# One small transfer from GpSimd's queue ahead of the setup of a fused attention and gated-MLP kernel

## The chip, the cores and the metric

The kernel runs on one core of a Trainium2 chip. The core has a matrix engine (TensorE, PE in the profile, with its weight loads as PEld), a vector engine (VectorE, DVE), an activation engine (ScalarE, ACT), a general engine (GpSimd, POOL) and a queue engine (SyncE, SP) that here only issues transfers. Each engine works through its own instructions in order and waits on semaphores for the others. Transfers run on 16 DMA engines; SP and ACT issue them on hardware queues, GpSimd on a software queue. The metric is the device time of one execution in microseconds, as the median of several runs; less is better.

## The reference

Layer norm, a sliding-window attention with dilation, a residual; layer norm, a ReLU-gated MLP, a residual. S = 2048 rows, D = 512, 32 heads of 16, window 8 with step 2, F = 1376, all in bfloat16:

```python
def _A_ref(x, wqkv, wo):
    qkv = (x @ wqkv).reshape(B, S, 3, H, Dh).transpose(2, 0, 3, 1, 4)
    q, k, v = qkv[0], qkv[1], qkv[2]
    idx = pos[:, None] - (jnp.arange(8) * 2)[None, :]
    ...
    logits = jnp.where(mask, jnp.einsum("bhsd,bhswd->bhsw", q, kg) * Dh ** -0.5, -1e9)
    o = jnp.einsum("bhsw,bhswd->bhsd", _softmax(logits), vg)
    return o.transpose(0, 2, 1, 3).reshape(B, S, D) @ wo

def _B_ref(x, W_gate, W_up, W_down):
    gate, up = x @ W_gate, x @ W_up
    return (gate * (gate > 0) * up) @ W_down

h = x + _A_ref(_layernorm(x), A_wqkv, A_wo)
out = h + _B_ref(_layernorm(h), B_W_gate, B_W_up, B_W_down)
```

## The kernel before

The 2048 rows are worked in four chunks of 512 (`tk`), each of four blocks of 128 rows (`j`). For each chunk: layer norm of x with rows on the partitions, transposes on PE (L518), projections to q, k, v with features on the partitions (L559, copied out by ACT at L567), products of q with the shifted k on DVE (L608, or L623 for the first chunk), their sums per head on PE (L614), exponentials on ACT, the weights spread to all partitions (over PE and ACT for the first chunk at L743 and L749, by SP's transfers at L732 for the others), products with the shifted v on DVE (L764, L779), a tree of sums of which the first level is an accumulating transfer of GpSimd's queue (L807, for chunks 0 to 2) and the rest is on DVE (L767, L771, L801), the output projection (L833), the second layer norm, gate and up (L906, L910, L913, L934) and down (L952, L963), and the store (L969).

The order of the work is fixed before the program is built. A planner class takes about 740 steps with an engine, an estimated duration and a rank from a table (`RANK`), lays them out and emits the instructions in that order, so that steps of several chunks interleave on each engine. No scheduler moves them afterwards; semaphore waits are placed between them by the framework.

Ahead of the planned steps stands `setup()`, in the order of its lines, and this is where the change lies:

- x of the first chunk is loaded in four transfers of 128 KB, by SP and ACT in turn (L309), then the q and k columns of the weights, `wqk_sb`, in four transfers of 256 KB (L311), one for each 128 of the 512 rows of `A_wqkv`; a row of that tensor has 3 x 512 elements, 3072 bytes. Then SP loads x of the second chunk (L312).
- DVE zeroes `warm` (L314). PE multiplies it 44 times into a bank that nobody reads (L408), and 8 times more after each of the first two transposed blocks (L416).
- GpSimd makes `identity` (two instructions of a helper), `eps_t` (L316), `ci`, the number of each partition (L317), four more index tables (L318 to L321) and the zero pads of `kT` and `vT` (L322, L323).
- GpSimd copies one element of x into `wv_sb` (L326) once the first x block has landed, which holds back SP's load of the v columns, `wv_sb` (L327), until then; a second copy of this kind (L328) holds back SP's loads of the other two x chunks (L330) and all weights behind them (L332 to L338) until x of the second chunk is there.
- DVE makes the constants `sel`, `spread`, `same` and `mask` from `ci` and the tables (L343 to L351).

After that come the planned steps, on DVE first those of the first layer norm: statistics of each x block (L454), their aggregate (L457), a logarithm and an exponential on ACT (L467, L471), the normalised rows (L489), a transpose on PE (L518), and a copy out of the bank by ACT (L534) or, for every second block, by DVE (L532). The first two projections to q and two to k run in halves: rows 0 to 255 of the weights against the first 256 x rows as soon as two blocks are copied out, and so on.

A transfer from GpSimd's queue is one instruction in GpSimd's order. Its landing is signalled on one of eight semaphores that these transfers use in turn.

Of the kernel before, what the change touches and what calls it, by code (L numbers as in the profile page):

```python
# [8 lines left out]
P = 128  # L9
BF16 = mybir.dt.bfloat16  # L10
# [81 lines left out]
class Plan:  # L92
# [9 lines left out]
    def add(self, key, *a, **k):  # L102
        op = Op(*a, **k)
        op.key = key
        op.seq = len(self.ops)
        if RANK:
            op.prio = RANK[op.seq]
        self.ops.append(op)
        for b in set(op.take) | set(op.use):
            b.left += 1  # L110
        return op
# [97 lines left out]
def kernel(  # L209
# [11 lines left out]
    nc = tc.nc  # L221
# [4 lines left out]
    NT = D // P  # L226
# [24 lines left out]
    sb = ctx.enter_context(tc.tile_pool(name="sb", bufs=1))  # L251
# [10 lines left out]
    mask = sb.tile([P, 2, PADL], BF16, name="mask")  # L262
    eps_t = sb.tile([P, 1], F32, name="eps_t")
    warm = sb.tile([P, P], BF16, name="warm")
    ci = sb.tile([P, 1], I32, name="ci")
    tmp = sb.tile([P, 3], I32, name="tmp")
    cf = sb.tile([P, 4], F32, name="cf")
# [37 lines left out]
    def setup():  # L305

        w3_r = A_wqkv.rearrange("(dt p) f -> p dt f", p=P)
        for j in range(BPC):
            (nc.scalar if j % 2 else nc.sync).dma_start(x_sm[:, j:j + 1, :], x_rows[:, j:j + 1, :])  # L309
        for dt in range(NT):  # L310
            (nc.scalar if dt % 2 else nc.sync).dma_start(wqk_sb[:, dt:dt + 1, :], w3_r[:, dt:dt + 1, 0:2 * D])  # L311
        nc.sync.dma_start(x_sm[:, BPC:2 * BPC, :], x_rows[:, BPC:2 * BPC, :])  # L312
        nc.scalar.preload_act_table_set("natural_log_exp_and_others")
        V.memset(warm[:], 0.0)  # L314
        make_identity(nc, identity[:])
        nc.gpsimd.memset(eps_t[:], EPS)  # L316
        nc.gpsimd.iota(ci[:], pattern=[[0, 1]], base=0, channel_multiplier=1)  # L317
        nc.gpsimd.iota(sel_i[:], pattern=[[1, H]], base=0, channel_multiplier=0)  # L318
        nc.gpsimd.iota(sp_i[:], pattern=[[1, H], [0, DQ]], base=0, channel_multiplier=0)
        nc.gpsimd.iota(sm_i, pattern=[[0, 4], [1, H]], base=0, channel_multiplier=0)  # L320
        nc.gpsimd.iota(mk_i[:], pattern=[[1, PADL]], base=0, channel_multiplier=0)  # L321
        nc.gpsimd.memset(kT[:, :, 0:PADL], 0.0)  # L322
        nc.gpsimd.memset(vT[:, :, 0:PADL], 0.0)  # L323


        nc.gpsimd.tensor_copy(out=wv_sb[0:1, 0, 0:1], in_=x_sm[0:1, 0, 0:1])  # L326
        nc.sync.dma_start(wv_sb[:], w3_r[:, :, 2 * D:3 * D])  # L327
        nc.gpsimd.tensor_copy(out=x_sm[0:1, 2 * BPC, 0:1], in_=x_sm[0:1, BPC, 0:1])  # L328
        for tk in range(2, NCK):
            nc.sync.dma_start(x_sm[:, tk * BPC:(tk + 1) * BPC, :], x_rows[:, tk * BPC:(tk + 1) * BPC, :])  # L330

        nc.sync.dma_start(wo_sb[:], A_wo.rearrange("(p t) f -> p t f", t=NT))  # L332
        nc.sync.dma_start(wgu_sb[:, :, 1, :], B_W_up.rearrange("(dt p) f -> p dt f", p=P))
        nc.sync.dma_start(wgu_sb[:, :, 0, :], B_W_gate.rearrange("(dt p) f -> p dt f", p=P))
        nc.sync.dma_start(
            wd_sb[:, 0:NFF, :], B_W_down[0:NFF * P, :].rearrange("(ft p) n -> p ft n", p=P))
        if FTAIL:
            nc.sync.dma_start(wd_sb[:FTAIL, NFF, :], B_W_down[NFF * P:F, :])  # L338


        for n, (op, by) in enumerate(((ALU.arith_shift_right, 2), (ALU.bitwise_and, H - 1),
                                      (ALU.arith_shift_right, 5))):
            V.tensor_scalar(out=tmp[:, n:n + 1], in0=ci[:], scalar1=by, scalar2=None, op0=op)  # L343
        V.tensor_copy(out=cf[:, 0:3], in_=tmp[:])
        V.tensor_scalar(out=cf[:, 2:3], in0=cf[:, 2:3], scalar1=1.0 * DIL, scalar2=None, op0=ALU.mult)
        V.tensor_scalar(out=cf[:, 3:4], in0=cf[:, 2:3], scalar1=4.0 * DIL, scalar2=None, op0=ALU.add)
        V.tensor_scalar(out=sel[:], in0=sel_i[:], scalar1=cf[:, 0:1], scalar2=None, op0=ALU.is_equal)
        V.tensor_scalar(out=spread[:], in0=sp_i[:], scalar1=cf[:, 1:2], scalar2=None, op0=ALU.is_equal)
        V.tensor_scalar(out=same[:], in0=sm_i, scalar1=cf[:, 1:2], scalar2=None, op0=ALU.is_equal)
        for hf in range(2):  # L350
            V.tensor_scalar(out=mask[:, hf, :], in0=mk_i[:], scalar1=cf[:, 2 + hf:3 + hf],  # L351
                            scalar2=None, op0=ALU.is_ge)
# [189 lines left out]
    for tk in range(NCK):  # L542
# [10 lines left out]
        for n, (c, t) in enumerate(seq):  # L553
# [16 lines left out]
            if tk == 0 and n < 4:  # L570

                ab, done = [wload["ab"]], []
                for i, (lo, hi, evs) in enumerate(((0, 2 * P, xev[0:2]), (2 * P, CS, xev[2:]))):
# [3 lines left out]
                a = add(("qkd%d" % n, tk), "PE", 2 * MM, lambda f=f_mm: f(0, CS, 2, NT), done + [wl], pr - 4.9, take=[mm],  # L577
                        use=[xnT], lat=PEL)
            else:
                a = add(("qkv%d" % n, tk), "PE", 4 * MM, f_mm, xev + [wl], pr, take=[mm], use=[xnT], lat=PEL)  # L580
# [13 lines left out]
        for hf in range(2):  # L594
            sc, ex = Buf(at_s), Buf(ex_s)
            scd, prd = [], []
            for t in range(0, NT, 2):
# [20 lines left out]
                if tk in PRS:  # L618
# [7 lines left out]
                    for u in range(2):  # L626
                        a = add(("pr%d%s" % (hf, "ac"[u]), tk), "DVE", D20, lambda u=u, f=f_p1: f(u),
                                [d[t + u] for d in (qd, kd, kp)], apr, take=[pb], use=[qT], lat=DL)
                        prd.append((a, pb, f_sc if u else lambda: None))
                else:  # L630
                    a = add(("pr%d" % hf, tk), "DVE", D40, f_pr, [d[k] for k in (t, t + 1) for d in (qd, kd, kp)],
                            apr, take=[pb], use=[qT], lat=DL)
                    prd.append((a, pb, f_sc))
            if (tk, hf) in PRD:
                def f_pd(p0=prd[0][1], p1=prd[1][1]):
                    nc.gpsimd.dma_start(p0.t[:], p1.t[:], accum_op=ALU.add, max_dma_last_dim=4096)

                a = add(("pd%d" % hf, tk), "POOL", 1.3, f_pd, [a for a, _, _ in prd], apr, use=[b for _, b, _ in prd],
                        lat=1.1, dq=(0.75, 5.48))
# [9 lines left out]
            elif (tk, hf) in PRE:  # L649
# [3 lines left out]
                a = add(("pa%d" % hf, tk), "DVE", D40, f_pa, [a for a, _, _ in prd], apr, use=[b for _, b, _ in prd], lat=DL)  # L653
# [24 lines left out]
            a = add(("ex%d" % hf, tk), "ACT", A5, f_ex, scd, apr, take=[ex], use=[sc], lat=AL)  # L678
            if tk == 0:
                a = add(("mk%d" % hf, tk), "DVE", DSM, f_mk, [a], apr, use=[ex], lat=DL)  # L680
# [41 lines left out]
        for w0 in range(0, W, BCN):  # L722
# [23 lines left out]
            a = add(("bc%d" % hf, tk), "PE", MM + SW, f_bc, [exd[hf]], apr + 1, take=bcs, use=[exs[hf]], lat=PEL)  # L746
# [9 lines left out]
        for t in range(NT):  # L756
# [46 lines left out]
            for n, du in ((4, D20), (2, D10), (1, D2)):  # L803
                f = lambda n=n, mt=mt, f=f_a: f(n, mt)
# [23 lines left out]
        for j in range(BPC):  # L828
# [10 lines left out]
            def f_rs(j=j, od=od, sm=sm, tk=tk):  # L839
# [3 lines left out]
                else:  # L843
# [3 lines left out]
            a = add(("wo%d" % j, tk), "PE", (5 if tk in RPE else 4) * MM, f_wo, list(oev.values()) + [wload["o"]],  # L847
                    base + 50, take=[od], use=[OT], lat=PEL)
            if tk in RPE:
                a = add(("rs%d" % j, tk), "ACT", 0.57, f_rs, [a], base + 50, take=[sm], use=[od], lat=AL)  # L850
            else:
                a = add(("rs%d" % j, tk), "DVE", 0.63, f_rs, [a], base + 50, take=[sm], use=[od], lat=DL)
# [7 lines left out]
        for f0 in range(0, NFT, 2):  # L860
            fts = range(f0, min(f0 + 2, NFT))
            if tk in TMT and fts[-1] == NFF:
# [4 lines left out]
                for b in range(2):  # L867
# [13 lines left out]
                    def f_tg(b=b, bk=bk, ht=ht, gr=gr):  # L881
# [4 lines left out]
                    a = add(("mm%d" % (f0 // 2), tk), "PE", 8 * TTM, f_tt, hev + [wload["u"], wload["g"]], mb + f0 * 0.1,  # L886
                            take=[bk], use=[hnT], lat=PEL)
                    a = add(("ge%d" % (f0 // 2), tk), "ACT", ATE, f_te, [a], mb + f0 * 0.1 - 200, take=[gr], use=[bk], lat=AL)
# [10 lines left out]
            for ft in fts:  # L899
# [15 lines left out]
                def mm(g, b, wl, pr=pr, f0=f0, ft=ft, f=f_mm, hnT=hnT):  # L915
                    if (tk, ft) not in HSP:
                        return add(("mm%d" % (f0 // 2), tk), "PE", 4 * MM, lambda: f(g, b), hev + [wload[wl]], pr,
                                   take=[b], use=[hnT], lat=PEL)
                    a = None
                    for i, (lo, hi, evs) in enumerate(((0, 2 * P, hev[0:1]), (2 * P, CS, hev[1:]))):  # L920
                        a = add(("mm%d%s" % (f0 // 2, "ac"[i]), tk), "PE", 2 * MM + 0.005, lambda lo=lo, hi=hi: f(g, b, lo, hi),
                                evs + [wload[wl], a], pr, take=[b], use=[hnT], lat=PEL if i else 0.0)
                    return a

                a = mm(1, um, "u")
# [11 lines left out]
            a = add(("gu%d" % (f0 // 2), tk), "DVE", D10 if n == 2 else D2, f_gu, eds, pr - 200, take=[gt], use=[ub, gr], lat=DL)  # L937
# [7 lines left out]
        for n, (j, c0, c1) in enumerate(parts):  # L945
# [25 lines left out]
            a = None  # L971
            for lo, hi in ((0, 8), (8, NFT)):
                a = add(("dn%d" % n, tk), "PE", (hi - lo + (hi == NFT and tk in OPE)) * MM * share,
                        lambda lo=lo, hi=hi, f=f_dn: f(range(lo, hi)),
                        [gds[ft] for ft in range(lo, hi)] + [wload["d"], a], mb + 5, take=[od],
                        use=[gts[ft] for ft in range(lo, hi)], lat=PEL if hi == NFT else 0.0)
# [5 lines left out]
    with tc.manual_schedule():  # L982
        setup()
        for op in todo:
            if op.fn is not None:
                op.fn()
# [35 lines left out]
```

## Time and profile before

| | |
|---|---|
| median of 3 runs | 198.1 us (198.0 to 198.31) |
| span of the profiled execution, first to last instruction | 196.6 us |
| PE busy | 190.5 us, 97% of the span |
| DVE busy | 154.0 us, 78% |
| ACT busy | 111.7 us, 57% |
| POOL busy | 12.7 us, 6% |
| DMA moved | 21.99 MB in 21134 packets, 112 GB/s on average |
| granted TensorE clock | 1.00 |

The profile is one execution; its span leaves out some 1.5 us that the timed runs have around it. An engine's busy time counts what it computes; POOL's also counts its issuing of transfers, which it does in software. A row of a time line has the start from the span's beginning, the duration, the engine, the line and what is written from what; the brackets tell how long the engine stood idle before and what ended that. A matmul is listed with its whole passage through the array, so rows overlap, and the pitch from one to the next is what it costs. Some matmul records, here 20 of 1131, are missing.

### The profile page before, as it was taken

The numbers are of one execution on the slowest core, as the hardware profiler recorded it, in microseconds if no ns is written. First come the engines' busy times: TensorE is split into PE (matmuls) and PEld (weight loads), VectorE is DVE, ScalarE is ACT, GpSimd is POOL, SyncE is SP. The second block draws the span as 40 slices with busy tenths as digits, with TensorE's granted clock in tenths as the row PEclk, the third lists the DMA queues.
The fourth block names the chain that finished last, engine by engine and source line by source line (L and its number), as shares of the span: only waits on it lengthen the run. The fifth ranks groups of instructions, "written<-read, shape, count | busy, mean of one in ns | idle before, by whom it ended". The sixth has DMA issues, their size and how long they took to land.

```text
span 196.6 us, 3034 instructions
## 1 busy us (share of the span) xinstructions
PE 190.5 (97%) x1111; PEld 97.1 (49%) x1131; DVE 154.0 (78%) x251; ACT 111.7 (57%) x234; POOL 12.7 (6%) x28
## 2 busy tenths in 40 slices
PE   7899999999999999999999999999999999999994
PEld 7756445654445434464444435444444655444542
DVE  6779999999999999999999779999686331223233
ACT  3548699984598947694334658505674615235400
POOL 4000000330000013100033000000000000000000
PEclk9999999999999999999999999999999999999999
DMA  6969980695000809947369971411002220030114
GB/s 154 310 202 389 405 262 2 122 198 108 3 0 6 196 15 173 188 89 169 81 130 198 181 204 64 82 29 24 3 0 53 53 57 0 0 107 0 27 57 133
DMA packets 21134, 21.99 MB, mean 112 GB/s; under 512 B 8736, under 2 KB 17920, under 8 KB 21120
## 3 DMA queue, kind: packets, MB, share of 16 engines
q1 hardware_dynamic: 18672, 14.65, 25.9%
q0 software_dynamic: 1728, 6.29, 17.2%
q10 hardware_dynamic: 720, 0.85, 1.4%
q8 instruction: 9, 0.15, 0.3%
q14 instruction: 5, 0.04, 0.1%
HBM read 8.42 MB, written 2.10 MB: 53 GB/s over the span
## 4 chain that ended last, share of the span: by engine, by line
PE 66%; DMA 14%; issue 13%; DVE 4%; POOL 1%; SPq 1%; POOLq 0%; DVEq 0%
PE bank L906 20%; PE bank L559 19%; PE bank L952 14%; DMA big<-big 7%; PE bank L833 5%; DMA wv_sb<-in_A_wqkv_dram 4%; PE bank L614 2%; DVE big L764 2%; PE bank L873 2%; PE bank L518 2%; DMA x_sm<-in_A_x_dram 1%; POOL big L807 1%; DMA big<-ex 1%; DVE big L608 1%; PE bank L836 1%
## 5 line engine op out<-in xcount | busy, mean ns | idle before, releaser
L906 PE MATMUL bank<-quad,wgu_sb 128*128 128x512 bf16 x313 | 72.0, 379 | 0.4
L906 PEld LDWEIGHTS <-wgu_sb 128*128 128x128 bf16 x320 | 31.0, 98 | 37.3 <-issue 0.8
L952 PE MATMUL bank<-wd_sb,gT 128*128 128x512 bf16 (+2 forms) x182 | 40.1, 366 | 0.3
L913 ACT ACTIVATE gr<-bank 128x512 bf16<-128x512 f32 x40 | 23.2, 603 | 26.0 <-PE bank L906 24.5
L910 ACT CAST up_sb<-bank 128x512 bf16<-128x512 f32 x40 | 23.2, 594 | 16.5 <-PE bank L906 14.0
L934 DVE TENSOR_TENSOR gT<-gr,up_sb 128x1024 bf16<-128x1024 bf16 x20 | 13.7, 689 | 22.7 <-ACT up_sb L910 16.8
L559 PE MATMUL bank<-quad,wqk_sb 128*128 128x512 bf16 (+1 forms) x132 | 30.2, 367 | 0.2
L952 PEld LDWEIGHTS <-gT 128*128 128x128 bf16 (+1 forms) x187 | 18.1, 98 | 19.5 <-issue 0.4
L764 DVE TENSOR_TENSOR big<-big,vT 128x4096 bf16<-128x4096 bf16 x12 | 27.0, 2283 | 0.1
L608 DVE TENSOR_TENSOR big<-quad,kT 128x4096 bf16<-128x4096 bf16 x12 | 27.0, 2284 | 0.0
L559 PEld LDWEIGHTS <-wqk_sb 128*128 128x128 bf16 x136 | 14.7, 114 | 13.0 <-issue 2.1
L963 DVE TENSOR_TENSOR row<-x_sm,bank 128x512 bf16<-128x512 bf16 (+1 forms) x17 | 10.8, 651 | 9.2 <-PE bank L952 9.2
L767 DVE TENSOR_TENSOR big<-big 128x1024 bf16<-128x1024 bf16 (+2 forms) x24 | 16.8, 729 | 1.2 <-DMA big<-big 1.2
L559 PE MATMUL bank<-quad,wv_sb 128*128 128x512 bf16 x62 | 15.7, 380 | 0.4 <-DMA wv_sb<-in_A_wqkv_dram 0.3
L807 POOL DMA_DIRECT2D big<-big x12 | 10.5, 874 | 85.0 <-DVE big L764 55.0
L833 PE MATMUL bank<-wo_sb,quad 128*128 128x512 bf16 x62 | 14.7, 379 | 0.4 <-DVE quad L801 0.3
L489 DVE TENSOR_SCALAR row<-x_sm,mv,rs 128x512 bf16<-128x512 bf16 x32 | 11.4, 407 | 1.8 <-ACT rs L471 1.8
L534 ACT COPY quad<-bank 128x1024 bf16<-128x1024 bf16 (+1 forms) x11 | 10.0, 944 | 4.5 <-PE bank L518 4.4
L567 ACT CAST kT<-bank 128x512 bf16<-128x512 f32 x16 | 8.9, 598 | 5.7 <-PE bank L559 5.5
L454 DVE BATCH_NORM_STATS2 st<-x_sm 128x6 f32<-128x512 bf16 x16 | 10.3, 675 | 2.1 <-DMA x_sm<-in_A_x_dram 2.1
L567 ACT CAST quad<-bank 128x512 bf16<-128x512 f32 x16 | 9.5, 607 | 3.6 <-PE bank L559 3.6
L443 ACT ACTIVATE row<-x_sm,mv 128x512 bf16<-128x512 bf16 x12 | 8.6, 714 | 4.2 <-DVE mv L435 4.0
(72 smaller groups left out, 157.5 us busy)
## 6 DMA issues: line engine op xcount, KB each, us to landing
big<-big POOLq DMA_DIRECT2D x12, 512.0 KB, 5.4
big<-ex SPq DMA_DIRECT2D x24, 128.0 KB, 2.7
out_dram<-row SPq DMA_DIRECT2D x15, 128.0 KB, 1.8
x_sm<-in_A_x_dram SPq DMA_DIRECT2D x3, 512.0 KB, 4.9
wgu_sb<-in_B_W_up_dram SPq DMA_DIRECT2D x1, 1376.0 KB, 8.8
wgu_sb<-in_B_W_gate_dram SPq DMA_DIRECT2D x1, 1376.0 KB, 11.8
wd_sb<-in_B_W_down_dram SPq DMA_DIRECT2D x1, 1280.0 KB, 15.2
wqk_sb<-in_A_wqkv_dram SPq DMA_DIRECT2D x2, 256.0 KB, 6.9
```

The lines of the kernel that those rows point to most:

```text
L559: nc.tensor.matmul(mm.t[:, lo:hi], lhsT=wv_sb[:, dt, t:D:NT] if c == 2 else wqk_sb[:, dt, c * D + t:(c + 1) * D:NT], rhs=xnT.t[:, dt, lo:h ...
L567: nc.scalar.copy(out=o, in_=mm.t[:])
L608: V.tensor_tensor(out=pb.t[:].rearrange("p (t w) s -> p t w s", t=2), in0=q4, in1=k4, op=ALU.mult)
L764: V.tensor_tensor(out=mt.t[:], in0=ab.t[:], in1=v8, op=ALU.mult)
L767: V.tensor_tensor(out=mt.t[:, 0:n, :], in0=mt.t[:, 0:n, :], in1=mt.t[:, n:2 * n, :], op=ALU.add)
L807: nc.gpsimd.dma_start(mt.t[:, 0:4, :], mt.t[:, 4:8, :], accum_op=ALU.add)
L833: nc.tensor.matmul(od.t[:], lhsT=OT.t[:, t, j * P:(j + 1) * P], rhs=wo_sb[:, t, :], start=(t == 0), stop=(t == NT - 1 and tk not in RPE))
L906: nc.tensor.matmul(mm.t[:fs, lo:hi], lhsT=wgu_sb[:, dt, g, ft * P: ft * P + fs], rhs=hnT.t[:, dt, lo:hi], start=(dt == 0), stop=(dt == NT ...
L910: nc.scalar.copy(out=ub.t[:fs, i, :], in_=um.t[:fs, :])
L913: nc.scalar.activation(out=gr.t[:fs, i, :], in_=gm.t[:fs, :], func=ACT.Relu)
L934: V.tensor_tensor(out=gt.t[:fs, 0:n, :], in0=gr.t[:fs, 0:n, :], in1=ub.t[:fs, 0:n, :], op=ALU.mult)
L952: nc.tensor.matmul(od.t[:, c0:c1], lhsT=gts[ft].t[:fs, ft % 2, j * P:(j + 1) * P], rhs=wd_sb[:fs, ft, c0:c1], start=(ft == 0), stop=(ft == ...
```

## The change

A tile `touch` of 128 partitions by 2 elements is added, and as the first instruction of `setup()` GpSimd issues a transfer into it: from each of the 128 groups of four rows of `A_wqkv` the first two elements of the first row, 4 bytes. The source rows are 12288 bytes apart and run over the whole tensor. Nothing reads `touch`. On GpSimd's queue the transfer stands ahead of `identity`; on the other engines the instructions and their order are the same. The new tile takes 32 bytes of each partition, so the tiles allocated after it lie 32 bytes higher. The later transfers of GpSimd's queue take the next of the eight semaphores each.

```diff
@@ -262,6 +262,7 @@
     mask = sb.tile([P, 2, PADL], BF16, name="mask")
     eps_t = sb.tile([P, 1], F32, name="eps_t")
     warm = sb.tile([P, P], BF16, name="warm")
+    touch = sb.tile([P, 2], BF16, name="touch")
     ci = sb.tile([P, 1], I32, name="ci")
@@ -305,6 +306,7 @@
     def setup():
 
         w3_r = A_wqkv.rearrange("(dt p) f -> p dt f", p=P)
+        nc.gpsimd.dma_start(touch[:], A_wqkv.rearrange("(p a) f -> p a f", a=NT)[:, 0, 0:2])
         for j in range(BPC):
             (nc.scalar if j % 2 else nc.sync).dma_start(x_sm[:, j:j + 1, :], x_rows[:, j:j + 1, :])
```

## The prediction

> **What bounds the kernel now.** I read the page first, for which engine is full; then the waits, for whether the full engine ever stands still; then the time lines of the first 14 us, engine by engine, because the only edit is the first instruction of GpSimd's queue.
>
> ```profile
> PE 190.5 (97%) x1111; PEld 97.1 (49%) x1131; DVE 154.0 (78%) x251; ACT 111.7 (57%) x234; POOL 12.7 (6%) x28
> PE   7899999999999999999999999999999999999994
> DVE  6779999999999999999999779999686331223233
> ```
>
> PE is full from the second slice (4.9 us each) to the end, DVE from the fourth to past 100 us. The first slices are the ramp: until the first projections PE runs matmuls on zeros (L408, L416) and a few transposes. From the waits, all that PE itself waits for in the run:
>
> ```profile
> PE bank L408 <- DVE warm L314: 1.0, 1, 1.0
> PE bank L518 <- DVE row L489: 0.6, 2, 0.3
> PE bank L833 <- DVE quad L801: 0.3, 1, 0.3
> PE bank L559 <- DMA wv_sb<-in_A_wqkv_dram: 0.3, 1, 0.3
> ```
>
> Columns: microseconds in total, times, longest. The first two are in the ramp. The last, before 12.22 us, is no wait: the block that begins at 8.76 us is 16 matmuls of 256 columns (0.109 apart) and 8 of 512 (0.216 apart), 3.47 us, so it ends at 12.23; the row below has 21 of the 24, the rest are missing records. So after 8.76 us PE never stands still but 0.33 us at 115.25. What sets the time is when the first projection starts, plus a block of PE work that has no holes. What sets that start is read on POOL, then DVE, then PE:
>
> ```profile
> 0.74 0.21 POOL masks.py:197 MEMSET identity<- 128x128 bf16 x1 [0.29 <-POOLq L1006]
> 1.30 0.14 POOL L317 IOTA ci<- 128x1 int32 x1
> 2.30 0.15 POOL L323 MEMSET vT<- 128x64 bf16 x1
> ...
> 34.72 1.01 POOL L807 DMA_DIRECT2D big<-big  x1 [23.65 <-DVE row L489]
> 37.11 0.86 POOL L807 DMA_DIRECT2D big<-big  x1 [1.38 <-PE bank L518]
> ```
> ```profile
> 1.47 0.27 DVE L343 TENSOR_SCALAR tmp<-ci 128x1 int32<-128x1 int32 x3 [0.54 <-POOL ci L317]
> ...
> 2.83 0.36 DVE L351 TENSOR_SCALAR mask<-big,cf 128x16 bf16<-128x16 int32 x2
> 3.37 0.69 DVE L454 BATCH_NORM_STATS2 st<-x_sm 128x6 f32<-128x512 bf16 x1 [0.17 <-DMA x_sm<-in_A_x_dram]
> ...
> 8.20 0.75 DVE L532 COPY quad<-bank 128x512 bf16<-128x512 bf16 x2
> 10.87 1.88 DVE L454 BATCH_NORM_STATS2 st<-x_sm 128x6 f32<-128x512 bf16 x3 [1.92 <-DMA x_sm<-in_A_x_dram]
> ```
> ```profile
> 8.33 0.40 PE L518 MATMUL bank<-identity,row 128*128 128x128 bf16 x4
> 8.76 3.21 PE L559 MATMUL bank<-quad,wqk_sb 128*128 128x256 bf16 x21
> ```
>
> (Columns: start, duration, engine, line, what; in brackets the idle time before it and what ended it.) POOL's constants run without a hole from 0.74 to 2.45. DVE stands until ci comes (1.44), makes the constants until 3.19, waits 0.17 for the first x rows, and is then full but for 0.30 us until the copy of the second transposed row block ends at 8.58, and that releases the first projection at 8.76. The weights for it (rows 0 to 255 of the q and k part) have landed at 8.31 in the semaphores of their two transfers, 0.27 earlier: close, but not last.
>
> **The change part by part.** *The transfer's hold on POOL.* It stands before the identity, so every POOL instruction of the setup moves behind it: identity, eps_t, ci, the four iotas, the two pads of kT and vT, and the copies L326 and L328. The trace has no small transfer on this queue; the nearest rows are the twelve L807 ones, also 128 rows each. From release to start each takes about half a microsecond, then 0.86 (first one 1.01) on POOL:
>
> ```profile
> 74.94 0.02 POOLq L807
> 74.96 0.47 issue
> 75.43 0.02 POOLq L807
> 75.45 0.86 POOL big L807
> ```
>
> So 0.51 + 1.01 (it will be the first of its queue) = 1.52 us. Bounds: below, nothing, if POOL hands the work on and goes to the memset at once (never seen: each L807 is followed by a wait of over 1 us); next, 0.86 if the half microsecond overlaps the start of the program; above, 0.57 + 1.01 = 1.58, the time from the wait's end (34.15) to the first L807's end. I take 1.52: same engine, same row count, first use.
>
> The Trainium skill bears on this: "DMA: Bandwidth & Descriptors", section "Anatomy of one DMA — SWDGE (gpsimd) path", puts most of the fixed 2 us into the receipt of the write at the end, and little into dispatch and descriptor generation; by it the estimated hold is about 0.1 us and the sum is nought. The rows above, with 0.86 us booked on POOL itself, speak against it, and I go by the rows.
>
> *What waits.* DVE's L343 is blocked on ci, and DVE takes its work in order, so behind it stand all constants, the statistics of the first four x blocks, their normalisation and both L532 copies. ci comes at 1.44 + 1.52 = 2.96, the constants end at 4.71, and the first statistics start there instead of at 3.37 (the 0.17 wait is used up): 1.52 - 0.17 = 1.35 us late. The rest of the stretch to 8.58 is DVE's own chain with ACT's logarithm and exponential inside it, all of which moves; the first projection starts at 8.76 + 1.35 = 10.11. The other POOL results have room: identity at 2.8 for a transpose at 6.1, eps_t at 2.8 for ACT at 4.4. L326 goes from 3.40 to about 3.97, so SP's wv load (L327) is issued some 0.15 later than 4.05; SP's older x load is still landing until 10.84 ahead of it, and wv is now wanted at 13.6, not 12.2. L328 waits for x at 10.89 as before.
>
> *The transfer itself.* 128 packets of 4 bytes beside 21134. They come after about 0.7 + 1.5 + 0.6 = 2.8 us (the first L807 ends at 35.73, its first packet is at 36.29), among the first x blocks, which land between 3.3 and 5.0. If they hold x up by less than 1.35 us the later DVE start covers it.
>
> *What it may give.* The load rate shows a stretch where the weights' first packets crawl:
>
> ```profile
> 3.00:3.50 0.50, 0.50 (x7) 0.50 (x6) 0.33 (x3) 0.50 (x1) 0.10 (x1) 1.00 1.04 363
> 4.50:5.00 0.50, 0.50 (x7) 0.50 (x6) 0.47 (x2) 0.38 (x2) 0.00 (x0) 1.00 1.18 166
> 5.00:5.50 0.50, 0.50 (x8) 0.50 (x6) 0.50 (x2) 0.36 (x2) 0.00 (x0) 1.00 0.75 139
> ```
>
> (Last two columns: DMA share, GB/s.) From 3.5 to 6.0 us the five half microseconds move 248, 172, 166, 139 and 205 GB/s where 363 is had before: engines taken, bytes missing. Against 363 that is 1.1 us of transfer. If touching the rows first cures it, q, k, v weights and the second x chunk land about 1.1 us sooner. I count it as nought: the first projection waits for DVE, not for weights, and DVE's 1.92 us of idling before 10.87 is room, not path.
>
> *Does the delay reach the end?* DVE regains it first: its idle 1.92 us swallows the 1.35, and its first product (L623, 13.46) had its operands 1.0 us earlier, so it starts only some 0.35 late. But PE has no hole to regain it in, and what DVE eats comes from PE through ACT; with the slack of each wait read from the trace, DVE is 1.2 us late again at 25 us. Only the 0.33 at 115.25 is left: there PE waits for DVE, whose L801 waits for a transfer of L807. If that chain is late by 1.02 or less, PE gives back 0.33; DVE just before it has small holes (0.87 and 1.16), so I let it.
>
> *Sum.* 1.52 - 0.17 - 0.33 = +1.02 us on a profiled span of 196.6, which becomes 197.6. The median of the runs, 198.1, is the span plus 1.5 us around it that this edit does not touch: 199.1.
>
> **The rivals.** *POOL is not held (not slower).* The transfer is handed on, the constants stay where they are, the weights land up to 1.1 us sooner. For it: POOL's time in the rows is booked roughly, and nothing was ever queued right behind a transfer; against it: 0.86 us of POOL in each. It decides when the hold is under 0.17 + 0.33 = 0.5 us. PE still starts at 8.76, since that waits for DVE; all there is to win is 0.33 at 115.25 through a DVE that gets its second x chunk sooner. 197.8 to 198.1; 197.9. (The Trainium skill's "DMA: Bandwidth & Descriptors", in the section named above, is on this side.)
>
> *Short hold.* Only 0.86 counts: 0.86 - 0.17 - 0.33 = 0.36, 198.5.
>
> *Nothing comes back at 115 us.* The L807 transfers there take 8.28 us beside SP's broadcasts; if they shift fully, the sum is 1.35: 199.5.
>
> *PE's clock.* The zero matmuls end at 5.87, and the transposes that followed at 6.12 now come at 7.47: a hole of 1.6 us where there was 0.25. In the trace they start 0.107 us apart up to 5.55 and the transposes 0.056 apart from 6.12, so full speed came after about 4.6 us of them. If the hole loses it, 4.6 us from 7.47 on are at half speed, to 12.07; of these the projections from 10.11 lose about 1.0 us: 200.1. Against it: PE is full again soon after. The Trainium skill, "TensorE: Matmul & The Clock Gate", Part 1, has the clock fall only after an idle window of about 3.4 us, and has windows that do not start with the kernel, so by it the hole is too short unless the first full window had not closed by 5.87; no run shown here tells.
>
> **How the numbers follow.** Full hold with the 0.33 given back: 0.48. Nothing given back: 0.13. Short hold: 0.10. POOL not held: 0.17. PE's clock: 0.08. Something faster that no row shows (every later tile moves by 32 bytes in SBUF): 0.04. The time is 199.1; its own range is 198.4 to 199.5. For eight in ten I go from the not-held case, 198.0, to just short of the clock case, 199.9. A change within 0.2% (0.4 us) is what a measurement of this kernel can't tell from none: slower 0.48 + 0.13 + 0.08 and half of the short hold, 0.74; same, the other half and most of the not-held case, 0.20; faster 0.06.
>
> **What would show it.** In the profile after: a POOL transfer near 1.2 us of 0.86 to 1.0; ci at about 2.9; the first L454 at about 4.7; the first L559 near 10.1, with PE full behind it; the wait of PE at 115 to 117 us gone; a span of 197.6. I'm wrong if the memset of identity starts before the transfer's row ends, if L559 starts near 8.8, or if the zero matmuls' successors are 0.107 us apart.

## The result, and the profile after

The changed kernel took 199.79 us (median of 4 runs, 199.46 to 200.1) and the kernel before, on the same chip, 198.2 us (median of 4, 198.0 to 198.41): a ratio of 1.0083, 95% interval 1.0068 to 1.0098. It is slower by 1.6 us. The profiled execution is the longest of the four, 200.1 us with a span of 198.0; the other three have spans of 197.4 to 197.8. In the experiments two executions at a mean granted clock of 0.86 and 0.76 (225.8 us in e4_consts_late_touch, 254.5 us in e6_more_warm) and one of the kernel before at 407.26 us are left out.

Lines of the changed kernel are one or two higher: L454 is L456 now, L489 is L491, L518 is L520, L532 is L534, L559 is L561, L833 is L835. First the page: busy times, and two rows of the span in 40 slices.

```profile
PE 192.0 (97%) x1131; PEld 97.8 (49%) x1131; DVE 154.2 (78%) x251; ACT 111.7 (56%) x234; POOL 13.2 (7%) x29
...
PE   7699999999999999999999999999999999999994
...
PEclk9789999999999999999999999999999999999999
```

PE's second slice (4.9 to 9.8 us) has gone from 8 to 6, and the granted clock shows a dip in the second and third. Everything behind looks as before. The loss is in the first 14 us, and it is followed along the same chain as in the prediction. GpSimd:

```profile
1.28 0.70 POOL L309 DMA_DIRECT2D touch<-in_A_wqkv_dram  x1 [0.84 <-POOLq L1008]
1.98 0.24 POOL masks.py:197 MEMSET identity<- 128x128 bf16 x1
2.29 0.29 POOL masks.py:199 TENSOR_SCALAR_AFFINE_SELECT identity<-identity 128x128 bf16<-128x128 bf16 x1
2.52 0.10 POOL L318 MEMSET eps_t<- 128x1 f32 x1
2.57 0.13 POOL L319 IOTA ci<- 128x1 int32 x1
```

Before, `identity` began at 0.74. It now waits for the transfer: 0.54 us until the transfer's row starts and 0.70 of the row, 1.24 in all. Vector, as a time line:

```profile
2.74 0.28 DVE L345 TENSOR_SCALAR tmp<-ci 128x1 int32<-128x1 int32 x3 [1.81 <-POOL ci L319]
...
4.38 0.69 DVE L456 BATCH_NORM_STATS2 st<-x_sm 128x6 f32<-128x512 bf16 x1
...
9.10 0.75 DVE L534 COPY quad<-bank 128x512 bf16<-128x512 bf16 x2
11.12 1.88 DVE L456 BATCH_NORM_STATS2 st<-x_sm 128x6 f32<-128x512 bf16 x3 [1.27 <-DMA x_sm<-in_A_x_dram]
```

The first statistics have lost their 0.17 us wait for x and start at 4.38 for 3.37 (+1.01); the copies that release the first projection start at 9.10 for 8.20 (+0.90). TensorE, as a time line of the same execution:

```profile
0.99 4.17 PE L410 MATMUL bank<-warm 128*128 128x128 bf16 x44 [0.99 <-DVE warm L316]
7.02 0.72 PE L520 MATMUL bank<-identity,row 128*128 128x128 bf16 x8 [1.86 <-DVE row L491]
7.58 0.96 PE L418 MATMUL bank<-warm 128*128 128x128 bf16 x8
8.53 0.61 PE L520 MATMUL bank<-identity,row 128*128 128x128 bf16 x4
8.93 1.06 PE L418 MATMUL bank<-warm 128*128 128x128 bf16 x8
9.79 0.63 PE L520 MATMUL bank<-identity,row 128*128 128x128 bf16 x4
10.21 3.64 PE L561 MATMUL bank<-quad,wqk_sb 128*128 128x256 bf16 x22
13.69 1.03 PE L561 MATMUL bank<-quad,wv_sb 128*128 128x512 bf16 x4
```

A hole of 1.86 us stands between the zero matmuls and the first transposes, and after it PE slows down: the second group of eight zero matmuls takes 1.06 us where the same line took 0.61 before. The first projection starts at 10.21 for 8.76 (+1.45), 0.55 more than its operands are late. The windows of the trace (length, PE busy and count, granted clock, DMA share, GB/s) have the edges of it:

```profile
7.25:7.65 0.40, 0.40 (x10) 1.00 0.87 292
7.70:8.20 0.50, 0.50 (x8) 0.50 1.07 381
10.60:11.05 0.45, 0.45 (x4) 0.50 0.27 96
11.10:11.60 0.50, 0.50 (x6) 1.00 0.21 74
```

Half clock from 7.68 to 11.09, 3.41 us. At 115 us, the waits and the time line:

```profile
PE bank L835 <- DVE quad L803: 0.3, 1, 0.3
```
```profile
116.61 1.68 PE L835 MATMUL bank<-wo_sb,quad 128*128 128x512 bf16 x7 [0.25 <-DVE quad L803]
```

PE reaches that line 1.36 us late (115.25 before), and the hole ahead of it is still there, 0.08 us shorter: next to nothing was given back.

The transfer was aimed at the load rate, and the profile after shows more of it from 3.5 to 6.0 us (length, busy times, clock, DMA share, GB/s):

```profile
3.50:6.00 2.50, 1.66 (x23) 1.49 (x20) 2.43 (x11) 0.92 (x3) 0.34 (x4) 1.00 0.83 247
```

Before it is 186. But this rate differs as much between executions without the transfer: 185 in e1, 260 in e5, and in e3, where only the tile is there:

```profile
3.50:6.00 2.50, 1.75 (x24) 1.58 (x22) 2.43 (x7) 1.42 (x5) 0.04 (x1) 1.00 0.93 254
```

So no effect of the transfer on the rate is shown. Nor did the weights come sooner here: the first half of the q and k weights lands at 8.33 and 8.52 us (8.13 and 8.31 before). In e10, the changed kernel again, it lands at 6.73 and 7.72, and in e9, which moves nothing, at 7.06 and 7.28.

### The profile page after: what moved, and what is told of

Same layout as the page of the kernel before. It is cut to its first block, busy times and chain, and to the rows that moved or that the text cites. A ratio compares the mean times of both kernels' runs of the same rounds, so it can differ in the third digit from the quotient of the medians.

```text
span 198.0 us, 3055 instructions
## 1 busy us (share of the span) xinstructions
PE 192.0 (97%) x1131; PEld 97.8 (49%) x1131; DVE 154.2 (78%) x251; ACT 111.7 (56%) x234; POOL 13.2 (7%) x29
## 2 busy tenths in 40 slices
DMA packets 21166, 21.99 MB, mean 111 GB/s; under 512 B 8768, under 2 KB 17952, under 8 KB 21152
## 4 chain that ended last, share of the span: by engine, by line
PE 69%; issue 13%; DMA 8%; DVE 6%; POOL 2%; SPq 0%; POOLq 0%; DVEq 0%
PE bank L561 21%; PE bank L908 20%; PE bank L954 14%; DMA big<-big 7%; PE bank L835 5%; PE bank L520 3%; PE bank L616 2%; DVE big L766 2%; PE bank L875 2%; POOL big L809 1%; DMA big<-ex 1%; PE bank L418 1%; DVE big L610 1%; DVE st L456 1%; PE bank L838 0%
## 5 line engine op out<-in xcount | busy, mean ns | idle before, releaser
L954 PE MATMUL bank<-wd_sb,gT 128*128 128x512 bf16 (+3 forms) x187 | 40.5, 367 | 0.0
L561 PE MATMUL bank<-quad,wqk_sb 128*128 128x512 bf16 (+1 forms) x136 | 30.8, 372 | 0.0
L561 PEld LDWEIGHTS <-wqk_sb 128*128 128x128 bf16 x136 | 15.0, 115 | 13.1 <-issue 1.9
L561 PE MATMUL bank<-quad,wv_sb 128*128 128x512 bf16 x64 | 15.8, 379 | 0.0
L835 PE MATMUL bank<-wo_sb,quad 128*128 128x512 bf16 x64 | 15.0, 379 | 0.3 <-DVE quad L803 0.3
L491 DVE TENSOR_SCALAR row<-x_sm,mv,rs 128x512 bf16<-128x512 bf16 x32 | 11.4, 406 | 1.7 <-ACT rs L473 1.7
L456 DVE BATCH_NORM_STATS2 st<-x_sm 128x6 f32<-128x512 bf16 x16 | 10.3, 674 | 1.3 <-DMA x_sm<-in_A_x_dram 1.3
```

The source lines that it names most:

```text
L456: V.bn_stats(out=st.t[:], in_=x_sm[:, tk * BPC + j, :])
L561: nc.tensor.matmul(mm.t[:, lo:hi], lhsT=wv_sb[:, dt, t:D:NT] if c == 2 else wqk_sb[:, dt, c * D + t:(c + 1) * D:NT], rhs=xnT.t[:, dt, lo:h ...
L835: nc.tensor.matmul(od.t[:], lhsT=OT.t[:, t, j * P:(j + 1) * P], rhs=wo_sb[:, t, :], start=(t == 0), stop=(t == NT - 1 and tk not in RPE))
L954: nc.tensor.matmul(od.t[:, c0:c1], lhsT=gts[ft].t[:fs, ft % 2, j * P:(j + 1) * P], rhs=wd_sb[:fs, ft, c0:c1], start=(ft == 0), stop=(ft == ...
```

## The experiments

The theory on trial (hold): GpSimd is busy with the transfer for 1.2 us, `ci` is late by that, and Vector's in-order queue carries it to the first projection. Its rivals: the 32 bytes that shift every later tile; the transfer itself, by what it does to queues and loads; and TensorE's clock, as cause of a part. The table has all twelve; each stands against the kernel before on the same chip. "Clock lost" counts the executions at a mean granted clock of 0.991, which is what 3.4 us at half clock make of 198 us; the others are at 0.998 or more. "Outside" is the mean of time less span. Diffs are against the changed kernel.

| kernel | median us (runs) | ratio, 95% interval | clock lost | median span | outside |
|---|---|---|---|---|---|
| before, on the three chips of the experiments | 198.15 to 198.32 (12 to 31) | | 0 | 196.3 to 196.5 | 1.78 to 1.81 |
| changed, first result | 199.79 (4) | 1.0083 [1.0068, 1.0098] | 1 | 197.7 | 2.08 |
| e10_after_again | 199.63 (6) | 1.0083 [1.0051, 1.0114] | 3 | 197.65 | 2.00 |
| e1_hold_only | 198.51 (10) | 1.0010 [0.9994, 1.0027] | 0 | 196.45 | 2.01 |
| e2_touch_behind | 198.66 (10) | 1.0019 [1.0001, 1.0036] | 0 | 196.65 | 2.03 |
| e3_tile_only | 198.27 (10) | 0.9995 [0.9978, 1.0012] | 0 | 196.45 | 1.79 |
| e4_consts_late_touch | 198.63 (9) | 1.0020 [1.0004, 1.0036] | 0 | 196.6 | 2.04 |
| e11, the same again | 198.39 (12) | 1.0012 [1.0001, 1.0022] | 0 | 196.4 | 2.02 |
| e5_consts_late_no_touch | 198.27 (11) | 0.9999 [0.9988, 1.0010] | 0 | 196.5 | 1.81 |
| e9_hold_long | 199.67 (7) | 1.0054 [1.0029, 1.0079] | 1 | 197.7 | 1.99 |
| e6_more_warm | 199.25 (3) | 1.0061 [1.0038, 1.0084] | 0 | 197.2 | 2.03 |
| e12, the same again | 199.28 (5) | 1.0067 [1.0054, 1.0080] | 0 | 197.3 | 2.04 |
| e7_two_touches | 200.87 (4) | 1.0145 [1.0121, 1.0169] | 4 | 198.65 | 2.26 |
| e8_touch_on_act | 199.66 (6) | 1.0081 [1.0049, 1.0113] | 2 | 197.85 | 1.81 |

**e1: a hold without a transfer.** The transfer is replaced by an index table that nobody reads; the tile stays.

```diff
-        nc.gpsimd.dma_start(touch[:], A_wqkv.rearrange("(p a) f -> p a f", a=NT)[:, 0, 0:2])
+        nc.gpsimd.iota(ints[:, 1024:1024 + 352], pattern=[[1, H], [0, 11]], base=0, channel_multiplier=0)
```

> The transfer is replaced by an index table of 352 numbers that nobody reads, written by GpSimd in its place; by the rows of the other tables it holds GpSimd for about 1.2 us, as the transfer did (identity from 0.74 to 1.98). Hold theory: the whole cost is GpSimd's hold on ci, so ci comes near 2.6, the first statistics start near 4.3 to 4.4, the first projection between 9.7 and 10.3, and the time is 1.0 to 1.6 us over the kernel before (ratio 1.005 to 1.008), like the changed kernel. Transfer theory: the 128 small reads are what costs, on the DMA side or around the span; then the time is within 0.4 us of the kernel before although the first statistics are late.

The table was too short to be the test it was meant for: it moved `identity` by 0.61 us, not 1.2. Its time, 0.2 us over the kernel before, therefore doesn't speak for the transfer theory. But it shows what half a hold does. PE, as a time line:

```profile
9.01 3.20 PE L561 MATMUL bank<-quad,wqk_sb 128*128 128x256 bf16 x22
12.22 1.05 PE L561 MATMUL bank<-quad,wv_sb 128*128 128x512 bf16 x4
```

The first projection starts 0.25 late and the v projection behind it not at all: it starts at 12.22, as before, because the v weights land at 12.18. The median span is the same as that of the kernel before on this chip (196.45 and 196.5).

**e2: the transfer behind GpSimd's constants.** The same transfer, after the pads.

```diff
-        nc.gpsimd.dma_start(touch[:], A_wqkv.rearrange("(p a) f -> p a f", a=NT)[:, 0, 0:2])
...
         nc.gpsimd.memset(vT[:, :, 0:PADL], 0.0)
+        nc.gpsimd.dma_start(touch[:], A_wqkv.rearrange("(p a) f -> p a f", a=NT)[:, 0, 0:2])
```

> The same transfer, issued by GpSimd behind its constants and pads and ahead of its copy of one x element into wv_sb. Hold theory: ci comes at 1.44 as before, the first statistics at 3.37, the first projection at 8.7 to 8.9; the copy into wv_sb ends near 3.9, in time for SP's load; the time is that of the kernel before within 0.2 us. Transfer theory: the reads still run among the first loads, x and the weights land later, and the time is 0.5 us or more over the kernel before.

GpSimd holds for it just as long, 0.72 us (time line), but with no constant behind it:

```profile
2.40 0.72 POOL L325 DMA_DIRECT2D touch<-in_A_wqkv_dram  x1
3.19 0.18 POOL L328 COPY wv_sb<-x_sm 1x1 bf16<-1x1 bf16 x1
```

Of the 1.6 us there is 0.34 left, and 0.23 of that lies outside the span. The transfer as such is cheap; its place is not.

**e3: the tile alone.** `touch` is allocated and nothing is loaded.

```diff
-        nc.gpsimd.dma_start(touch[:], A_wqkv.rearrange("(p a) f -> p a f", a=NT)[:, 0, 0:2])
```

> The tile of 32 bytes stays, the transfer goes. Hold and transfer theories: the kernel before, within 0.2 us. Address theory (the later tiles lie 32 bytes higher and transfers or engines are slower for it): some or all of the 1.6 us stays, and the rows of L809, L734 or L456 have longer means than 861, 2.7 and 675.

No difference. The 32 bytes are out.

**e4, e11 and their control e5: the transfer first, but nothing urgent waiting.** Vector's constants (L343 to L351 of before) are put into a function and emitted behind the two L532 copies, into Vector's idle stretch before 10.87; e5 does the same and leaves out the transfer; its tile stays.

```diff
+    def consts():
...
+        late = True
...
+            if late and op.key and op.key[0].startswith("xst") and op.key[1] == 1:
+                consts()
+                late = False
```

> The transfer stays ahead of all on GpSimd; DVE makes its constants only after the two copies out of the transposes, in the 1.9 us in which it waits for the second x chunk. Hold theory: nothing early waits for ci any more, the first statistics start near 3.4, the first projection near 8.8, the hole between the zero matmuls and the transposes is back to 0.3 us, and the time is that of the kernel before within 0.3 us. Transfer theory: x lands late or the weights do, so the first projection starts after 9.2 and the time is 0.5 us or more over the kernel before.

> DVE's constants made late as in the fourth kernel, without the transfer: the control for it. All theories: the kernel before within 0.3 us; first statistics when x lands, 3.2 to 3.4; first projection 8.4 to 8.8.

> The fourth kernel again, beside its control. Hold theory: the same as the control within 0.2 us, since nothing early waits for GpSimd. Transfer theory: 0.3 us or more over the control. Warming theory (the reads bring the weights sooner): the last q, k part and the v part land 0.5 us or more before the control's, and the time is the control's or less.

In e11 the transfer stands where the change put it and holds GpSimd as long (0.71 us, `ci` at 2.58), yet the first projection starts at 8.76, exactly as before, because Vector no longer waits for `ci` (time line):

```profile
8.76 3.20 PE L563 MATMUL bank<-quad,wqk_sb 128*128 128x256 bf16 x22
11.80 1.03 PE L563 MATMUL bank<-quad,wv_sb 128*128 128x512 bf16 x4
```

The cost of the change is gone but for 0.21 us, and that lies outside the span (2.02 against 1.81; median spans 196.4 and 196.4). The last line shows a gain, too: the v weights landed at 11.66 in this execution, and the v projection starts 0.42 sooner than before. The median spans of e11 and e5 (196.4, 196.5) leave little of it, so a gain is not shown.

**e9: a hold of the right length, no transfer.** As e1, with a table that takes longer.

```diff
-        nc.gpsimd.dma_start(touch[:], A_wqkv.rearrange("(p a) f -> p a f", a=NT)[:, 0, 0:2])
+        nc.gpsimd.iota(ints[:, 1024:1024 + 312], pattern=[[1, 78], [0, 4]], base=0, channel_multiplier=0)
```

> As the first hold without a transfer, but of a shape (78 numbers, each four times) whose cost, by the two tables measured so far (14 ns for each number, 0.3 ns for each element), is about 1.2 us, that of the transfer. Hold theory: identity near 1.98, first statistics near 4.4, first copy out by DVE near 9.1, and the time is 0.9 to 1.6 us over the kernel before, the same as the changed kernel beside it. Transfer theory: it stays under half of what the changed kernel costs.

```profile
0.84 1.02 POOL L309 IOTA big<- 128x312 int32 x1 [0.39 <-POOLq L1008]
...
2.36 0.13 POOL L319 IOTA ci<- 128x1 int32 x1
```

`ci` is 1.06 late instead of 1.27, with not one byte moved, and the time is 199.67, beside 199.63 of the changed kernel on the same chip (e10); the intervals of the two ratios overlap. The median is of two groups, 198.69 to 198.84 (three) and 199.67 to 199.9 (four); the mean of its runs is 199.36, that of e10's 199.74. GpSimd's being busy is enough for most of the loss, and within the spread of the runs for all of it. PE in this execution, which lost the clock, as a time line:

```profile
6.81 0.90 PE L520 MATMUL bank<-identity,row 128*128 128x128 bf16 x8 [1.87 <-DVE row L491]
...
13.38 1.03 PE L561 MATMUL bank<-quad,wv_sb 128*128 128x512 bf16 x4
```

**e10, e6, e12: the clock.** e10 is the changed kernel again; e6 and e12 have 66 zero matmuls instead of 44, so that PE has no hole before the transposes.

```diff
-    NWARM, NFILL = 44, 8
+    NWARM, NFILL = 66, 8
```

> The changed kernel once more, on the chip of the three others, as their measure: 0.9 to 1.9 us over the kernel before. Clock theory: the profiles in which PE loses half its clock after the hole are the slow ones of its runs, by 0.4 to 0.6 us.

> The changed kernel with 66 instead of 44 zero matmuls at the start, so that the hole ahead of the first transposes shrinks from 1.9 to about 0.6 us. Clock theory: PE keeps its full clock in every profile, the first projection comes about 0.9 us later than in the kernel before and not 1.45, and the time is 0.3 to 0.6 us under the changed kernel's. Hold theory alone: no difference to the changed kernel. If the zero matmuls end after 7.0 they push the transposes, and it is slower.

> The changed kernel with 66 zero matmuls again, for the spread of its times: clock theory: all undisturbed times lie within 0.7 us of each other, 0.6 to 1.4 us over the kernel before, with none of the upper group that the changed kernel showed (199.0 to 199.2 and 200.1 to 200.6). Without it, a second group a microsecond higher appears here as well.

e10's six runs are two groups: 198.97 to 199.18 at a clock of 0.999 or more, 200.08 to 200.62 at 0.991. Their medians are 1.58 apart, where 0.4 to 0.6 was expected. Its profile fell into the first. PE in it, as a time line:

```profile
0.99 4.88 PE L410 MATMUL bank<-warm 128*128 128x128 bf16 x44 [0.99 <-DVE warm L316]
7.03 0.72 PE L520 MATMUL bank<-identity,row 128*128 128x128 bf16 x8 [1.16 <-DVE row L491]
7.58 0.61 PE L418 MATMUL bank<-warm 128*128 128x128 bf16 x8
...
9.67 3.20 PE L561 MATMUL bank<-quad,wqk_sb 128*128 128x256 bf16 x22
12.71 1.03 PE L561 MATMUL bank<-quad,wv_sb 128*128 128x512 bf16 x4
```

One program, two executions: here the zero matmuls end 0.71 later, the hole is 1.16 us, the clock stays, and the v projection starts at 12.71 instead of 13.69. That 0.98 us is what the clock costs between these two; their spans differ by 0.8. With the hole filled no run of eight lost the clock and none was above 199.75; PE in e12 (time line) starts its projections at the same times as e10:

```profile
7.53 0.61 PE L520 MATMUL bank<-identity,row 128*128 128x128 bf16 x8
...
9.67 3.21 PE L561 MATMUL bank<-quad,wqk_sb 128*128 128x256 bf16 x22
12.71 1.03 PE L561 MATMUL bank<-quad,wv_sb 128*128 128x512 bf16 x4
```

What remains there, 1.1 us in both, is the change without the clock.

**e7: two transfers.** A second tile takes elements 2 and 3 of the same rows.

```diff
+        nc.gpsimd.dma_start(touch2[:], A_wqkv.rearrange("(p a) f -> p a f", a=NT)[:, 0, 2:4])
```

> The transfer twice, one behind the other, into two tiles. Hold theory: each holds GpSimd for 1.2 us or, if only the 0.70 of its row counts for the second, 0.7 to 1.2; identity at 2.7 to 3.2, first statistics 0.7 to 1.2 later than in the changed kernel (5.1 to 5.6), and the time another 0.7 to 1.3 us over it. With the hole before the transposes at 2.6 to 3.1 us the clock is lost more often. Transfer theory (reads in cold memory): the second finds the rows touched, so it adds under 0.3 us.

```profile
1.29 0.71 POOL L310 DMA_DIRECT2D touch<-in_A_wqkv_dram  x1 [0.85 <-POOLq L1010]
1.99 0.58 POOL L311 DMA_DIRECT2D touch<-in_A_wqkv_dram  x1
2.53 0.25 POOL masks.py:197 MEMSET identity<- 128x128 bf16 x1
```

The second holds GpSimd 0.55 us more, and all four runs lost the clock. Against the four runs of the changed kernel that lost it too (200.08 to 200.62, median 200.34), 200.87 is 0.53 more. Both figures are less than the hold theory expected (0.7 or more), and the time is more than the 0.3 of the transfer theory.

**e8: the transfer on Scalar's queue.** GpSimd is not held.

```diff
-        nc.gpsimd.dma_start(touch[:], A_wqkv.rearrange("(p a) f -> p a f", a=NT)[:, 0, 0:2])
+        nc.scalar.dma_start(touch[:], A_wqkv.rearrange("(p a) f -> p a f", a=NT)[:, 0, 0:2])
```

> The same 128 reads, but issued by ACT on its hardware queue ahead of its x loads, so GpSimd holds nothing back and the reads start near 1.8 us, 1.7 before the first weight packet (from GpSimd they started at 3.3, with the weights). Hold theory: ci at 1.44; only ACT's own queue is 0.45 late, so x blocks 1 and 3 land up to 0.5 later than before, the first statistics stay at 3.2 to 3.4, the first projection is at 8.5 to 9.2, and the time is 0 to 0.5 us over the kernel before. Warming theory: the slow stretch of the loads from 3.5 to 6.0 us goes, the weights' transfers land 0.8 us or more earlier (the q, k parts by 7.5 and 8.9 instead of 8.3 and 9.7). If they don't, the reads warm nothing.

It costs the same, against 0 to 0.5 us expected, by another road: `touch` goes ahead of Scalar's x loads, and one of its x blocks comes only at 6.09 us. Vector (time line):

```profile
6.11 0.70 DVE L456 BATCH_NORM_STATS2 st<-x_sm 128x6 f32<-128x512 bf16 x1 [1.10 <-DMA x_sm<-in_A_x_dram]
```

Here the weights did come much sooner, the first at 5.91 instead of 8.13 and the v columns at 10.90 instead of 12.17, with 297 GB/s from 3.5 to 6.0 us; e9, without a transfer, has 7.06 and 11.28. It did not pay: the first projection waits for Vector, at 10.36 in this execution, which lost the clock too. One profile; that this is the earlier reading of the rows is not shown.

No kernel tried was faster than the one before.

## Why the prediction was right, and where not

The direction, the mechanism and the range (198.0 to 199.9) held; the forecast of 199.1 was 0.7 us low. By its steps:

- *GpSimd is held.* Right, and shown: the hold alone costs about as much (e9), the transfer where nothing waits for it costs 0.2 to 0.4 (e2, e4, e11), and Vector's wait for `ci` is the link (e11 against the change). The Trainium skill, "DMA: Bandwidth & Descriptors", section "Anatomy of one DMA — SWDGE (gpsimd) path", by which the hold was estimated at 0.1 us, is not borne out: 1.24 us here.
- *1.52 us of hold.* Mis-sized: 0.54 + 0.70 = 1.24. The half microsecond was right; the row of this transfer is shorter than the L807 rows taken for it (0.86 to 1.01), with as many rows of partitions but 4 bytes in each.
- *Less the 0.17 wait for x.* Right in kind: 1.24 became 1.01 at the first statistics, 0.90 at the copies and 0.91 at the first projection of e10.
- *"The last, before 12.22 us, is no wait."* Wrong. It took the block ahead of the v projection for 24 matmuls. There are 22, which the profiles of e10 and e11 both list: 16 x 0.109 + 6 x 0.216 = 3.04 us, and e11 runs it in just that, 8.76 to 11.80. So PE stood 0.42 us before 12.22, waiting for the v weights that landed at 12.17. This hole takes up 0.42 of the delay: e10's first projection is 0.91 late, its v projection 0.49; e1's are 0.25 and nought. For the same reason an earlier landing of the weights was not worth nought, as the prediction counted it because the first projection waits for Vector: the v projection waits for weights.
- *PE gives back 0.33 at 115.25.* Wrong: the hole is 0.25 in the profile after and 0.41 in e10. The whole chain of L807 transfers and of Vector moved with PE (the transfer that ends the wait starts at 107.18, before at 105.74), which was the rival "nothing comes back".
- *1.5 us around the span that this edit doesn't touch.* Wrong twice. It is 1.8 before; the profiled span of 196.6 was a little over the median span, 196.3 to 196.5. And it grows: 1.99 to 2.08 with one more instruction on GpSimd, 2.26 with two, 1.81 with the transfer on Scalar.
- *PE's clock,* the rival at 0.08, priced at 1.0 us on top. The price was right for the two executions with a trace, 0.98, though it was reckoned from 4.6 us at half clock from 7.47 on, and it was 3.41 from 7.68 on; the chance was far too small: at least 4 of the 10 runs of the changed kernel lost it. The Trainium skill, "TensorE: Matmul & The Clock Gate", Part 1, by which a hole needs about 3.4 us, is not borne out for a hole in the first full window: 1.68 to 1.87 us were enough (e8, e7, the profile after, e9). The length of its window is: the half clock lasts 3.41.
- *Two smaller readings,* in no sum: the page of the profile after counts 32 packets more (21166), not 128, and the shortfall of the load rate is 1.2 us by the prediction's own five figures, not 1.1.

Put together for a run that keeps the clock: 0.91 - 0.42 + 0.22 = 0.71 us; e10's three such runs have a median of 198.99, 0.84 over 198.15. With the clock lost, 0.98 more: 1.69, but e10's other three are 2.4 over; 0.7 of that is not accounted for. That the forecast came near has some luck in it: a hold too long by 0.28 and a hole of 0.42 that was missed made it too high, a give-back that did not come (0.33) and two costs that were not counted, 0.22 outside the span and the clock, made it too low.

What stays open: three runs of the first result count as having kept the clock and still took 199.46 to 199.85, three of e9 took 199.67 to 199.9 and one of e8 200.1; they left no trace. "Kept" has a limit: the mean granted clock leaves out what lies before full speed is first reached. In e12 the zero matmuls run 0.107 us apart until 6.99 us, and the mean is 1.000 all the same. An execution in which full speed first comes behind the hole would run its first projections at half speed and still count as having kept the clock. That these seven are such executions fits e6 and e12, where the hole is filled and no time is above 199.75, but it is not shown.

Spans of the kernel before spread as well, 195.8 to 197.2. In the thirteen profiles other than e4's the span ends 184.2 to 184.8 us after the v projection starts, whatever the kernel; so what moves that start moves the time. The landing of the v weights is one such thing: PE waited for it until 11.85 in e2, 12.22 before and 12.45 in e3, and the spans are 196.1, 196.6 and 196.8.

## What to carry to other kernels

Ahead of this queue's first urgent instruction there was no free place: a transfer of 512 bytes on GpSimd held it 1.24 us, and what counted was not the transfer but which engine's in-order queue waited for the tables behind it. Before a wait in the profile is put down to missing records, count the instructions ahead of it in the engine's own order. Where a change opens a hole in PE's warm-up, price the clock with it, and look at several executions, since one profile shows only one of the two outcomes.

## What the runs showed of the hardware

- The clock fell 3.41 us after full speed was first reached, if PE had stood still for about half of that stretch. In e9 full speed came at 3.79 (the pitch of the zero matmuls halves), the hole was 1.87 us and the half clock ran from 7.21 to 10.62. In e11 it came at about the same time, the hole was 1.21, and the clock stayed; in e10 it came at 5.73, two holes of 1.16 and 0.34 add up to 1.50, and it stayed. e7: full at 5.94, holes of 1.73 and 0.34, half clock from 9.35 to 12.77. When full speed first comes differs from run to run (3.7 to 6.7 us with 44 zero matmuls), and since the 44 zero matmuls end sooner where it comes early, the hole itself differs: 1.16 in e10, 1.86 in the profile after.
- Each instruction added to GpSimd, transfer or table, first or last of the setup, adds 0.2 us to the time outside the span: 1.78 to 1.81 without (before, e3, e5, e8), 1.99 to 2.08 with one (nine rows of the table), 2.26 with two (e7). What takes it is open.
- A table's price is set by its pattern and not by its size: 352 elements as 32 x 11 took 0.56 us, 312 as 78 x 4 took 1.02.
